# A three-stage kernel (attention, FFN, top-1 MoE): transposes moved to TensorE and to earlier places, row gathers issued a step ahead, another order of weight conversions and scatters

## The chip, the cores and the metric

The kernel runs on one core of a Trainium2 chip. The metric is the device time of one execution in microseconds (us). The figure for the kernel before is the median of three runs; the profile is of one execution, whose own time stands beside it below. Engines go by the profile's names: PE (TensorE), DVE (VectorE), ACT (ScalarE), POOL (GpSimd) and SP (SyncE, which only issues DMAs here).

## What is computed

```python
# 1. attention, 16 heads x 768 rows x 64; a row sees only keys of its own LSH bucket
scores = np.where(q_bucket[..., :, None] == k_bucket[..., None, :], q @ k.T / 8, -1e9)
x = softmax(scores) @ v                     # rearranged to 1536 tokens x 512

# 2. FFN, 512 -> 2048 -> 512, with a rational activation
h = x @ w_in
g = P3(h) / (1 + abs(b0) * abs(h) + abs(b1) * h * h + 1e-6)
x = g @ w_out

# 3. top-1 mixture of 8 experts, 512 -> 1024 -> 512
e_idx = np.argmax(x @ w_gate, axis=1)
gate_w = softmax(x @ w_gate)[rows, e_idx]
eom = sigmoid(x @ w_output_gate)
for e in range(8):
    mask = e_idx == e
    out[mask] = gate_w[mask, None] * eom[mask, e, None] * (np.maximum(x[mask] @ w1[e], 0) @ w2[e])
```

Which token goes to which expert is known only on the chip, after the last FFN tile.

## The kernel before

**Numbers.** Float32 matmuls are made of float16 parts: each operand is split into a high and a low half, and three products (high by high, high by low, low by high) are added up. Weights of the MoE arrive as float32 chunks of 128x1024 (512 KB) in eight buffers `st`. ACT converts a chunk into its high half `WH` (`conv_hi`, L1003), DVE then makes the low half `WL` (`conv_lo`, L1006). One expert has eight chunks, four for the up projection and four for the down projection.

**FFN.** Twelve tiles of 128 tokens go through `ffn_unit` and `ffn_end` (L663 to L679). `ffn_end` scales the result and splits it into halves (`X`, L667 on ACT, L668 on DVE), has it transposed by a DMA of SP (`x2T`), writes it to a scratch tensor `x2d`, and computes the gate logits on PE (L676, copied to `LG` by DVE, L679).

**Routing.** From the logits, `gating`, `early` and `final` give each token a slot. Slots are sorted by expert and lie in *pairs* of 2 x 128 rows (up to 12) and *rests* of 64 rows (up to 7). `inv(0)` on PE turns slots into row indices, DVE copies them as `idg` (for gathers, L936) and `idx` (for scatters). `SR` with numbers 1 and 2 (L940) and two more `inv` do the same for the scale of each row. Small one-row passes on DVE (L945 to L966) make registers and flags: which expert each pair and rest has, which pairs need new weights, how many pairs and rests there are. PE, SP, ACT, DVE and POOL load these flags. With this data there are 6 pairs (0 to 5) and 4 rests (0 to 3), and among the pairs after the first the expert changes once, at pair 4.

**Order.** All of the work up to pair 0 and the gather and transpose of pair 1 is a graph of operations; where each one stands is written down in the table `PLACES` (two characters for each operation), and the engines execute in that order. What follows, `tail`, is issued in the order in which its code is written. Each engine works strictly in its own order, so an instruction that waits holds up all that stand behind it on its engine.

**The tail.** Step `k` (1 to 5 here) works on pair `k` and rest `k-1`:

- POOL gathers rows of `x2d` into `XG` (L985): pair `k+1` and rest `k`. SP transposes `XG` to `XGT` (pairs) or `XRT` (rests) by DMA (L988).
- PE computes the hidden layer of the pair: `mm1` (L1020) for pairs 0 and 1, `up_pair` (L1078) for the others. ACT and DVE apply relu and split it into halves of `HT` (L1083, L1084). PE computes the output in `mm2s` (L1035). ACT scales it to `OS` (`scale_out`, L1039), POOL scatters it to the rows of `out` (`scatter`, L1043).
- SP loads the next weights (L792): the chunks of rest `k` by `load_rest`, and those of pair `k+1` by `load_pair` (its chunks are moved only if that pair's expert differs). ACT and DVE convert rest `k-1`'s chunks (`conv_rest`) between the pair's relus, and pair `k+1`'s in `renew`, under a flag.
- PE computes the rest in `rest(k-1)` (L1095 and L1108, relu `HTR` at L1098), and POOL scatters it (L1113).

In `step`, the gathers for the next step are issued at its start; in `whole(k)` the transposes stand between the two halves of `up_pair` (`turns(k)`), and the scatters of the pair stand at the end, after the next step's flag is known.

## Time and profile before

| | |
|---|---|
| median of 3 runs | 669.41 us (666.66, 669.41, 671.71) |
| profiled execution | 669.22 us, of which the span of the profile is 667.4 us |
| TensorE's granted clock, mean | 0.985 of full speed |
| busy: PE / DVE / ACT / POOL | 580.8 / 557.8 / 438.8 / 273.2 us |

The span runs from the first to the last instruction that the profiler recorded; 1.8 us of the execution lie outside. A clock of 1.00 is 2.4 GHz, one of 0.50 is 1.2 GHz. In a list of waits, the engine and line that waited stand first, and behind the arrow what ended the wait. In a timeline, brackets hold the idle time of the engine before an instruction.

### The profile page before, as it was taken

What the parts mean: (1) busy time and instruction counts of PE and PEld (TensorE: products, weight loads), DVE (VectorE), ACT (ScalarE), POOL (GpSimd) and SP (SyncE); (2) the same over time, 40 slices, a digit from 0 to 9 for tenths busy, and PEclk for the clock granted to TensorE, in tenths of its full rate; (3) what the DMA queues carried; (4) which work ended last, traced back from release to release, by engine and by line L of the source; (5) the groups of instructions that cost most, each with busy time, mean ns of one, the idle gap of its engine ahead of it and who ended that gap; (6) DMA issues with size and microseconds to landing.
All of it is one profiled execution on the core that took longest, in us unless ns stands there. A gap on an engine that the chain in (4) does not pass through costs nothing.

```text
span 667.4 us, 18493 instructions
## 1 busy us (share of the span) xinstructions
PE 580.8 (87%) x7243; PEld 419.3 (63%) x7243; DVE 557.8 (84%) x1183; ACT 438.8 (66%) x644; POOL 273.2 (41%) x219
## 2 busy tenths in 40 slices
PE   0129997999999999999899999999997969979993
PEld 0015786677777776777676777777575746737571
DVE  6999999999999999988999999999965357176652
ACT  4417769988887887888877877765811356176552
POOL 1000215676656736664656564631303103121431
PEclk9999999999999999999999999999999979979997
DMA  8877889998899999999879995744813886799535
GB/s 267 245 228 232 220 237 197 176 166 170 134 158 180 196 211 175 155 165 164 145 134 155 154 149 89 130 95 97 276 35 101 227 227 226 155 396 329 172 90 111
DMA packets 224147, 119.62 MB, mean 179 GB/s; under 512 B 201647, under 2 KB 206639, under 8 KB 224048
## 3 DMA queue, kind: packets, MB, share of 16 engines
q1 hardware_dynamic: 221296, 109.92, 75.4%
q0 software_dynamic: 2752, 8.39, 4.1%
q8 instruction: 60, 0.98, 0.6%
q14 instruction: 39, 0.32, 0.2%
HBM read 80.01 MB, written 6.82 MB: 130 GB/s over the span
## 4 chain that ended last, share of the span: by engine, by line
DVE 37%; DMA 20%; issue 16%; ACT 12%; PE 11%; POOL 3%; POOLq 0%; SPq 0%; DVEq 0%; ACTq 0%
DMA out<-OS,idx 10%; DVE sm L568 7%; DMA pT<-phl 5%; ACT p L576 3%; DVE tmp L648 3%; ACT phl L312 3%; DVE tmp L440 2%; PE bank L660 2%; DVE tmp L649 2%; DVE WL L443 2%; DVE tmp L441 2%; DVE tmp L650 2%; DVE tmp L653 2%; DVE tmp L655 2%; DVE bank L654 2%
## 5 line engine op out<-in xcount | busy, mean ns | idle before, releaser
L313 POOL TENSOR_TENSOR phl<-p,phl 128x768 f16<-128x768 f32 x80 | 135.9, 1706 | 87.0 <-ACT phl L312 42.4
L634 PE MATMUL bank<-XT,WH 128*128 128x128 f16 x1440 | 129.6, 219 | 2.1 <-DVE tmp L655 1.5
L634 PEld LDWEIGHTS <-WH 128*128 128x128 f16 x1536 | 119.9, 98 | 15.2 <-issue 2.7
L634 PE MATMUL bank<-XT,WL 128*128 128x128 f16 x720 | 124.9, 219 | 0.2 <-DVE sm L569 0.2
L576 ACT ACTIVATE p<-scb,sm 128x768 f32<-128x768 f32 x96 | 93.0, 986 | 21.3 <-DVE sm L570 13.6
L660 PE MATMUL bank<-WH,G 128*128 128x512 f16 x352 | 104.9, 379 | 0.0
L568 DVE TENSOR_REDUCE sm<-scb 128x1 f32<-128x768 f32 x96 | 90.3, 950 | 4.6 <-PE scb L562 3.1
L660 PEld LDWEIGHTS <-G 128*128 128x128 f16 x576 | 52.2, 97 | 51.1 <-POOL G L313 1.4
L1006 DVE SCALAR_TENSOR_TENSOR WL<-st,WH 128x1024 f16<-128x1024 f32 x56 | 66.8, 1233 | 20.3 <-ACT WH L1003 18.3
L634 PEld LDWEIGHTS <-WL 128*128 128x128 f16 x768 | 75.1, 98 | 0.3 <-DVE WL L443 0.3
L313 POOL TENSOR_TENSOR G<-tmp,G 128x512 f16<-128x512 f32 x39 | 46.9, 1205 | 60.4 <-ACT G L312 56.4
L1003 ACT ACTIVATE WH<-st 128x1024 f16<-128x1024 f32 x56 | 56.5, 1049 | 21.6 <-DMA st<-in_w 21.3
L660 PE MATMUL bank<-WL,G 128*128 128x512 f16 x176 | 66.7, 379 | 0.0
L1035 PE MATMUL bank<-WH,HT 128*128 128x512 f16 x192 | 59.8, 392 | 5.8 <-ACT HT L1083 3.8
L312 ACT ACTIVATE phl<-p 128x768 f16<-128x768 f32 x72 | 60.1, 839 | 6.9 <-DMA pT<-phl 6.0
L585 PE MATMUL bank<-VH,pT 128*128 128x65 f16 x528 | 55.2, 195 | 2.9 <-DMA pT<-phl 2.5
L586 PE MATMUL bank<-VL,pT 128*128 128x64 f16 x528 | 55.2, 192 | 0.0
L587 PE MATMUL bank<-VH,pT 128*128 128x65 f16 x528 | 55.1, 193 | 0.0
L585 PEld LDWEIGHTS <-pT 128*128 128x128 f16 x528 | 49.1, 97 | 8.7 <-DMA pT<-phl 4.8
L1035 PEld LDWEIGHTS <-HT 128*128 128x128 f16 x288 | 28.2, 100 | 40.6 <-issue 4.3
L562 PE MATMUL scb<-AK,AQ 128*128 128x384 f16 x192 | 46.8, 326 | 5.8 <-ACT p L576 5.2
L586 PEld LDWEIGHTS <-pT 128*128 128x128 f16 x528 | 48.9, 99 | 4.6 <-issue 0.7
(282 smaller groups left out, 1425.2 us busy)
## 6 DMA issues: line engine op xcount, KB each, us to landing
st<-in_w SPq DMA_DIRECT2D x92, 512.0 KB
tmp<-in_wio SPq DMA_DIRECT2D x32, 512.0 KB
qraw<-in_qt_ SPq DMA_DIRECT2D x12, 256.0 KB
x2d<-X SPq DMA_DIRECT2D x12, 256.0 KB
kraw<-in_kt_ SPq DMA_DIRECT2D x5, 384.0 KB
vr<-in_v SPq DMA_DIRECT2D x5, 384.0 KB
AQ<-BQ SPq DMA_DIRECT2D x24, 64.0 KB
pT<-phl SPq DMA_TRANSPOSE x88
```

The costliest lines, as they stand in the source:

```text
L312: g.op("ACT", c_act(n, 1), lambda: nc.scalar.activation(out=hi, in_=src, func=AF.Copy), r=rd, w=kh, prio=prio, tag=tags[0], alt=[("DVE", c ...
L313: f = lambda e: lambda: e.tensor_tensor(out=lo, in0=src, in1=hi, op=ALU.subtract)
L568: g.op("DVE", 0.865, lambda: nc.vector.tensor_reduce(out=s[:, 0:1], in_=sc, axis=AX.XY, op=ALU.max), r=kb, w=[("mx", ks)], prio=prio, tag= ...
L576: g.op("ACT", 0.975 if ac else 0.885, lambda: nc.scalar.activation(out=pf.rearrange("p (c n) -> p c n", c=2), in_=sc, func=AF.Exp, bias=s[ ...
L585: nc.tensor.matmul(o, lhsT=pt[:, k], rhs=VH[p][:, hh, k], start=(k == 0), stop=False)
L586: nc.tensor.matmul(o[:, 0:D], lhsT=pt[:, k], rhs=VL[p][:, hh, k], start=False, stop=False)
L587: nc.tensor.matmul(o, lhsT=pt[:, 6 + k], rhs=VH[p][:, hh, k], start=False, stop=(k == 5))
L634: nc.tensor.matmul(hp[:, j * 128:j * 128 + 128], lhsT=w_[:, f, d * 128:d * 128 + 128], rhs=xt[:, hl * 4 + d], start=(k == 0), stop=(k == 11))
L660: nc.tensor.matmul(bank_f32(abank), lhsT=G_[:, gl, c0:c0 + 128], rhs=w_[:, f, 512:1024], start=(f == 0 and k == 0), stop=(f == FT - 1 and ...
L1003: nc.scalar.activation(out=P["W"][p][0][c], in_=P["st"][c], func=AF.Copy, scale=512.0)
L1006: nc.vector.scalar_tensor_tensor(out=P["W"][p][1][c], in0=P["st"][c], scalar=512.0, in1=P["W"][p][0][c], op0=ALU.mult, op1=ALU.subtract)
L1035: nc.tensor.matmul(bank_f32(6 + sub), lhsT=P["HT"][sub][:, hl, f], rhs=w_[4 + f // 2][:, c0:c0 + 512], start=(f == 0 and n == 0), stop=(f ...
```

## The change

It has five parts.

1. In `ffn_end` the last tile's halves are transposed by eight matmuls against the identity matrix (four into bank 1, evicted by ACT, four into the accumulator's bank, evicted by DVE) instead of a DMA of SP.
2. `idg` becomes an input of the two products `SR` 1 and 2 and of the first of the small passes that make flags, so that the row indices come first on DVE; one relu of pair 0 is put behind `SR` 0.
3. Pair 1's gathered rows are transposed by TensorE (`turn_pe`, evicted by `turned`) instead of SP.
4. In the tail, gathers are issued one step further ahead (`fetch(k + 2, k + 1)` in `turns(k)`), the transposes of the next pair stand at the start of a step, and rest 0's loads stand ahead of its gather and transposes. Half 0's relus come before the first three conversions of a rest, half 1's after them; conversions 3 to 7 follow those. The scatters of a pair directly follow its scaling, ahead of the rest's scatter. From step 5 on each half is scaled and scattered when its `mm2s` are done. The branch that held only the last scatters is gone.
5. Four rows of `PLACES` are new, for the order of the graph part.

```diff
 PLACES = (
...
-    "z{z}!0!2!4!6!8wEw)wWxBv3v{wkvfwuw|uqwYx9vNwmxjwOxLx=v}w@x^u!w~xZvzxFxzxNxVxbxfxpx/xrxxx[x}y4yAy2yCyGyayoyyy:y~zFzTyKyMyOySygyuxlzBzRzXzd!Gzhzp!E!I!O!Q!S!U!a!ezn!W!K!i"
...
+    "z{z}!0!2!4!6!8!A!C!EwMxHwmx*v3v{w+vfw|xluqwox(vNw:yKwax^yqv}xbywu!xpyAvzx=yax{y6yCyGyQymySyYyuy$y<y@y:y]y|z9zHzNzRzXzdzhz1z3z5z7zDzLyMzbzfzjzl!Szpzv!Q!U!a!c!e!g!k!ozt!G!I!K!W"
...
-        g.op("SP", TR, lambda: nc.sync.dma_start_transpose(out=x2T[i], in_=x2.rearrange("p a b -> p (a b)")), r=[("X2h", i), ("X2l", i)], w=[("x2T", i)], dma=1.27, prio=pr, tag="xz")
+        kx2 = [("x2T", i)] if ti < TILES - 1 else [("x2T", i, hl) for hl in range(2)]
+        if ti < TILES - 1:
...
+        else:
+            for hl, b in ((0, 1), (1, abank)):
+                def tu(hl=hl, b=b):
+                    for d in range(4):
+                        nc.tensor.matmul(bank_f32(b)[:, d * 128:d * 128 + 128], lhsT=x2[:, hl, d * 128:d * 128 + 128], rhs=P["ident"], start=True, stop=True)
...
-        g.op("DVE", 0.42, lambda k=k: V.tensor_tensor(out=P["SR"][:, k], in0=P["SO"], in1=bc(VAL[:, :, k:k + 1], [128, TILES, NSLOT]), op=ALU.mult), r=["SO"] + [(kk, b_) for b_ in blks], w=[("SR", k)], prio=RT2)
+        g.op("DVE", 0.42, lambda k=k: V.tensor_tensor(out=P["SR"][:, k], in0=P["SO"], in1=bc(VAL[:, :, k:k + 1], [128, TILES, NSLOT]), op=ALU.mult), r=["SO", "idg"] + [(kk, b_) for b_ in blks], w=[("SR", k)], prio=RT2)
...
+    def turn_pe(sub):
+        for c in range(8):
+            nc.tensor.matmul(scb[c // 4][:, sub, 128 * (c % 4):128 * (c % 4) + 128], lhsT=P["XG"][2 + sub][:, c], rhs=P["ident"], start=True, stop=True)
+
+    def turned(sub, h):
+        o, b = P["XGT"][2 + sub][:, 4 * h:4 * h + 4].rearrange("p a b -> p (a b)"), scb[h][:, sub]
+        if h:
+            nc.vector.tensor_copy(o, b)
+        else:
+            nc.scalar.activation(out=o, in_=b, func=AF.Copy)
...
-        g.op("SP", TR, lambda sub=sub: turn(1, sub), r=[("XG", 2 + sub)], w=[("XGT", 2 + sub)], dma=1.27, prio=RT + 49)
+        if not sub:
+            g.op("PE", c_mm(128, 8), lambda: turn_pe(0), r=[("XG", 2), "ident"], w=[bkey(2), bkey(4)], prio=RT + 49)
...
+        def out_of(k, sub):
+            scale_out(k, sub), scatter(k, sub)
+
+        def first_pair():
+            for sub in range(2):
+                for half in range(2):
+                    mm1(1, sub, half)
+                    if not sub and not half:
+                        turn_pe(1), turned(1, 0), turned(1, 1)
+                        fetch(2, 1), turns(1)
+                    relu_hi(1, sub, half), relu_lo(1, sub, half)
+                conv_rest(0, 4 * sub, 4 * sub + 4)
+                load_pair(2, 4 * sub, 4 * sub + 4)
+
         def whole(k):
-            r = k - 1
-            if k > 1:
-                conv_rest(r, 0, 4)
-                load_pair(k + 1, 0, 4)
-                up_pair(k, 0)
-                turns(k)
-                up_pair(k, 1)
-            else:
...
-            conv_rest(r, 4, 8)
-            load_pair(k + 1, 4, 8)
-            for sub in range(2):
-                for half in range(2):
-                    mm2s(k, sub, half)
+            r, late = k - 1, k > 4
+            if k == 1:
+                first_pair()
+            else:
+                up_pair(k, 0)
+                conv_rest(r, 0, 3), load_pair(k + 1, 0, 3)
+                up_pair(k, 1)
+                conv_rest(r, 3, 4 if late else 8), load_pair(k + 1, 3, 4 if late else 8)
+            mm2s(k, 0, 0), mm2s(k, 0, 1)
+            if late:
+                out_of(k, 0)
+                conv_rest(r, 4, 8), load_pair(k + 1, 4, 8)
+            mm2s(k, 1, 0), mm2s(k, 1, 1)
+            if late:
+                out_of(k, 1)
+            else:
+                scale_out(k, 0)
...
+        def fetch(k, r):
+            if k < NB:
+                gather(k, 0), gather(k, 1)
+            if r < NR:
+                gather_rest(r)
+
         def turns(k):
             if k + 1 < NB:
                 turn(k + 1, 0), turn(k + 1, 1)
             if k < NR:
                 turn_rest(k)
+            fetch(k + 2, k + 1)
...
         def step(k):
             r = k - 1
-            if k + 1 < NB:
-                gather(k + 1, 0), gather(k + 1, 1)
             if k == 1:
-                gather_rest(0), turn_rest(0)
                 load_rest(0, 0, 8)
-            if k < NR:
-                gather_rest(k)
+                gather_rest(0)
+                turn_rest(0)
+            else:
+                turns(k)
...
             renew(k + 1, 0, 4)
             load_rest(k, 0, 4)
-            scale_out(k, 0), scale_out(k, 1)
+            if k < 5:
+                scale_out(k, 1)
+                scatter(k, 0), scatter(k, 1)
...
         def steps_from(k):
             step(k)
             if k + 1 == NB:
-                scatters(k)
-            elif k < 4:
-                load_rest(k, 4, 8), scatters(k), steps_from(k + 1)
-            else:
-                with tc.If(steps > k + 1) as more:
-                    load_rest(k, 4, 8), scatters(k), steps_from(k + 1)
-                with more.Else():
-                    scatters(k)
+                return
+            with tc.If(steps > k + 1) if k > 3 else ExitStack():
+                load_rest(k, 4, 8), steps_from(k + 1)
```

How this moves instructions, at three places. First SP, from its load of the flags (`fli`) to the first loads of rest 0 (`st` from `in_w1`, `regs` being the registers that name the expert). Before:

```order
L970 TENSOR_LOAD fli_7400
L970 ISA x8
L988 DMA_TRANSPOSE XGT1_7435<-XG2_7430 128x8x128
L988 DMA_TRANSPOSE XGT1_7435<-XG3_7431 128x8x128
L988 DMA_TRANSPOSE XRT0_7436<-XG4_7432 128x8x128
L978 TENSOR_LOAD regs_7397
L978 ISA x2
L978 TENSOR_LOAD regs_7397
L978 ISA x2
L792 ISA
L792 DMA st0_7420<-in_w1 128x1024
```

After:

```order
L983 TENSOR_LOAD fli_7400
L983 ISA x8
L991 TENSOR_LOAD regs_7397
L991 ISA x2
L991 TENSOR_LOAD regs_7397
L991 ISA x2
L805 ISA
L805 DMA st0_7420<-in_w1 128x1024
```

The two transposes of pair 1 (`XGT1`) are gone from SP, and that of rest 0 (`XRT0`) has moved from ahead of the eight loads to behind them.

Then POOL, from pair 0's second scatter on (`XG2` and `XG3` hold a pair's gathered rows, `XG4` and `XG5` a rest's; the L1043 and L1067 rows behind it are the scatters of pair 1). Before:

```order
L1043 DMA out_0<-OS1_7442,idx0_7383 1536x512
L985 DMA XG2_7430<-x2d_72,idg_7391 128x1024
L985 DMA XG3_7431<-x2d_72,idg_7391 128x1024
L985 DMA XG4_7432<-x2d_72,idg_7391 128x1024
L985 DMA XG5_7433<-x2d_72,idg_7391 128x1024
L1148 REGISTER_ALU
L1148 COMPARE_AND_BRANCH
L1148 UNCONDITIONAL_BRANCH x2
L1201 COMPARE_AND_BRANCH
L1113 DMA out_0<-OS2_7443,idx_7390 1536x512
```

After:

```order
L1067 DMA out_0<-OS1_7442,idx0_7383 1536x512
L998 DMA XG4_7432<-x2d_72,idg_7391 128x1024
L998 DMA XG2_7430<-x2d_72,idg_7391 128x1024
L998 DMA XG3_7431<-x2d_72,idg_7391 128x1024
L998 DMA XG5_7433<-x2d_72,idg_7391 128x1024
L998 DMA XG2_7430<-x2d_72,idg_7391 128x1024
L998 DMA XG3_7431<-x2d_72,idg_7391 128x1024
L998 DMA XG4_7432<-x2d_72,idg_7391 128x1024
L1169 REGISTER_ALU
L1169 COMPARE_AND_BRANCH
L1169 UNCONDITIONAL_BRANCH x2
L1067 DMA out_0<-OS0_7441,idx_7390 1536x512
```

Three more gathers (pair 3 and rest 2) now stand in step 1, and pair 1's scatters ahead of the rest's scatter.

Last ACT in step 2 (`WH` from `st` are conversions, `HT` from `scb0` and `scb1` the relus of `up_pair`'s halves 0 and 1). Before:

```order
L1003 ACTIVATE WH_148<-st0_7420 128x1024
L1003 ACTIVATE WH_148<-st1_7421 128x1024
L1003 ACTIVATE WH_148<-st2_7422 128x1024
L1003 ACTIVATE WH_148<-st3_7423 128x1024
L1083 ACTIVATE HT_7438<-scb0_70 128x512 x2
L1083 ACTIVATE HT_7438<-scb1_71 128x512 x2
L1003 ACTIVATE WH_148<-st4_7424 128x1024
L1003 ACTIVATE WH_148<-st5_7425 128x1024
L1003 ACTIVATE WH_148<-st6_7426 128x1024
L1003 ACTIVATE WH_148<-st7_7427 128x1024
```

After:

```order
L1110 ACTIVATE HT_7438<-scb0_70 128x512 x2
L1027 ACTIVATE WH_148<-st0_7420 128x1024
L1027 ACTIVATE WH_148<-st1_7421 128x1024
L1027 ACTIVATE WH_148<-st2_7422 128x1024
L1110 ACTIVATE HT_7438<-scb1_71 128x512 x2
L1027 ACTIVATE WH_148<-st3_7423 128x1024
L1027 ACTIVATE WH_148<-st4_7424 128x1024
L1027 ACTIVATE WH_148<-st5_7425 128x1024
L1027 ACTIVATE WH_148<-st6_7426 128x1024
L1027 ACTIVATE WH_148<-st7_7427 128x1024
L1063 ACTIVATE OS0_7441<-bank6_68,cs__7394 128x512
```

The relus of half 0 have moved ahead of all conversions, those of half 1 ahead of the fourth only.

## Rows read from the trace of the kernel before

**Rows 1.** The page, part 1: busy time, share of the span, instructions of each engine.

```profile
PE 580.8 (87%) x7243; PEld 419.3 (63%) x7243; DVE 557.8 (84%) x1183; ACT 438.8 (66%) x644; POOL 273.2 (41%) x219
```

**Rows 2.** Waits of PE, 440 to 668 us: total, times, longest, in us.

```profile
PE scb L1108 <- ACT HTR L1098: 5.0, 1, 5.0
PE bank L1035 <- ACT HT L1083: 3.8, 1, 3.8
PE scb L1020 <- DMA XGT<-XG: 2.3, 1, 2.3
```

**Rows 3.** Timeline of PE: start, us, instructions [idle before, releaser].

```profile
497.62 0.20 PE L676 MATMUL bank<-wgh,x2T 128*128 128x16 f16 x2
...
514.18 0.27 PE L1020 MATMUL scb<-XGT,WH 128*128 128x128 f16 x2 [2.27 <-DMA XGT<-XG]
...
535.25 0.22 PE L1095 MATMUL bank<-XRT,WH 128*128 128x64 f16 x2
...
548.24 0.39 PE L1078 MATMUL scb<-XGT,WH 128*128 128x256 f16 x2
...
574.69 0.39 PE L1078 MATMUL scb<-XGT,WH 128*128 128x256 f16 x2
...
608.73 0.39 PE L1078 MATMUL scb<-XGT,WH 128*128 128x256 f16 x2
...
636.24 0.39 PE L1078 MATMUL scb<-XGT,WH 128*128 128x256 f16 x2
...
656.23 0.38 PE L1035 MATMUL bank<-WL,HT 128*128 128x512 f16 x1
...
656.88 0.38 PE L1035 MATMUL bank<-WL,HT 128*128 128x512 f16 x1
```

**Rows 4.** Windows: length; busy PE, PEld, DVE, ACT, POOL; PEclk, DMA share, GB/s.

```profile
514.00:524.00 10.00, 9.82 (x176) 9.82 (x176) 2.08 (x3) 1.79 (x3) 4.03 (x4) 1.00 0.75 163
540.00:550.00 10.00, 6.77 (x41) 3.52 (x42) 2.73 (x4) 4.33 (x7) 0.00 (x0) 0.66 0.66 179
...
590.00:600.00 10.00, 9.63 (x33) 3.91 (x34) 8.42 (x10) 8.51 (x10) 1.67 (x2) 0.72 1.04 389
```

**Rows 5.** Timeline of ACT: a conversion in step 3, the last scaling.

```profile
600.24 1.06 ACT L1003 ACTIVATE WH<-st 128x1024 f16<-128x1024 f32 x1 [0.23 <-DMA st<-in_w]
...
657.34 0.69 ACT L1039 ACTIVATE OS<-bank,cs__7394 128x512 f32<-128x512 f32 x1 [3.74 <-PEq L1201]
```

**Rows 6.** Waits of SP's queue, 500 to 668 us: total, times, longest.

```profile
SPq L988 <- DMA XG<-x2d,idg: 46.2, 11, 10.5
```

**Rows 7.** Timeline of SP's queue: start, us, instructions.

```profile
510.87 2.67 SPq L988 DMA_TRANSPOSE XGT<-XG  x2
...
525.21 10.96 SPq L792 DMA_DIRECT2D st<-in_w  x12
...
574.74 15.33 SPq L792 DMA_DIRECT2D st<-in_w  x16
...
650.86 3.75 SPq L988 DMA_TRANSPOSE XGT<-XG  x2
```

**Rows 8.** Timeline of DVE: the last tile's low half, its logits, row indices, flags.

```profile
492.85 0.69 DVE L668 SCALAR_TENSOR_TENSOR X<-scb,X 128x512 f16<-128x512 f32 x1 [1.12 <-ACT X L667]
...
498.11 0.17 DVE L679 COPY LG<-bank 128x16 f32<-128x16 f32 x1 [3.14 <-PE bank L676]
...
506.53 0.19 DVE L936 TENSOR_SCALAR idg<-bank 128x31 int32<-128x31 f32 x1
...
508.20 0.28 DVE L966 CAST fli<-flc 1x4 int32<-1x4 f32 x1
```

**Rows 9.** Timeline of POOL: the last two scatters.

```profile
653.88 1.57 POOL L1043 DMA_INDIRECT out<-OS,idx  x1 [3.40 <-ACT OS L1039]
661.72 1.00 POOL L1043 DMA_INDIRECT out<-OS,idx  x1 [6.27 <-DMA out<-OS,idx]
```

**Rows 10.** Tile `OS`: time from issue to landing of its scatters.

```profile
DMA to landing us min/median/max: 2.0/3.3/7.1
```

More of the change, by code (lines that the diff above doesn't have):

```diff
@@ L677, in gm @@
                     k += 1
-        g.op("PE", c_mm(16, 12), gm, r=[("x2T", i), "wgh", "wgl"], w=[kPV], prio=pr)
+        g.op("PE", c_mm(16, 12), gm, r=kx2 + ["wgh", "wgl"], w=[kPV], prio=pr)
         g.op("DVE", 0.11, lambda: nc.vector.tensor_copy(LG[:, ti, :], GT), r=[kPV], w=[("LG", ti)], prio=pr)
@@ L1136, in conv_rest, with renew, whole, without @@
                 conv(1, c0, c1)
+        f_new, n_rest, n_pair, steps = flags
+        def renew(k, c0, c1):
+            if k < NB:
+                with tc.If((f_new & (1 << (k - 1))) > 0):
+                    conv(0, c0, c1)
+        def out_of(k, sub):
[10 more added lines that the diff above has]
+                load_pair(2, 4 * sub, 4 * sub + 4)
+        def whole(k):
+            r, late = k - 1, k > 4
[15 more added lines that the diff above has]
+                scale_out(k, 0)
+        def without(k):
+            conv_rest(k - 1, 0, 8)
+            load_pair(k + 1, 0, 8)
+        def fetch(k, r):
+            if k < NB:
+                gather(k, 0), gather(k, 1)
+            if r < NR:
+                gather_rest(r)
         def turns(k):
```

42 lines of the change are left out of this document (16 added, 26 removed).

## The prediction, made before the changed kernel was run

> **What bounds the kernel now.** I read the page first. TensorE is busy for 580.8 us of a span of 667.4 us [rows 1], so what matters is where it stands idle and where it runs slowly. The program is the same in both kernels up to the end of the last FFN tile, about 492 us into the span, so only the last 175 us can change. There I read the waits of TensorE [rows 2]: three waits stand out, 5.0 us on a relu of a rest (`HTR`), 3.8 us on a relu of a pair (`HT`) and 2.3 us on the transposed rows of pair 1 (`XGT`). Next the starts of the steps on TensorE's timeline [rows 3]. A step lasts from one pair's first matmul to the next one's: step 1 from 514.18 to 548.24 = 34.06 us, step 2 26.45, step 3 34.04, step 4 27.51, step 5 20.8 (to the last matmul at 656.88, and 0.2 more), then 10.3 us to the end of the span. Steps 1 to 4 hold the same matmuls, so step 2 shows what a step costs with nothing in the way, and steps 1 and 3 lose 7.6 us each. The windows [rows 4] say how: 5.0 us of step 1's excess is the wait, and most of the rest is the granted clock, 0.66 in 540 to 550 us and 0.72 in 590 to 600 us (a mixture of 1.2 and 2.4 GHz), so both idle times are followed by a stretch at half clock. After the wait of 2.27 us ahead of 514.18 the clock stayed at 1.00.
>
> Why TensorE waits is on ScalarE: the relus stand behind weight conversions, and these wait for `st`, that is for loads [rows 5]. The loads are issued by SP, in order, behind the transposes of gathered rows, and SP waited for gathers 46.2 us in 11 waits [rows 6]. Rest 0's first load is issued at 525.21, 11 us into its step; the loads for step 3 wait until 574.74, when step 3 has already begun [rows 7]. So the bound of this stretch is the start of the loads. The end of the span is bound by something else: the scatter issued at 653.88 has to land before the next can start, at 661.72, and that waits 6.27 us for it [rows 9].
>
> **The change, part by part.** All sums are made against the profiled run (span 667.4, run 669.22: 1.8 us lie outside the span). Its time is 0.2 us under the median of the three runs, 669.41.
>
> *Start: last tile, indices first, first pair by TensorE.* The last tile's transposition leaves SP: its low half is ready at 493.54 and its logits are copied at 498.11 [rows 8], 4.57 us. After: eight matmuls of 128 columns (176 such took 9.82 us [rows 4], so 0.45), two copies of 128x512 side by side (0.69 [rows 5]), three matmuls of mm2s that stand ahead of the gating on TensorE (656.23 to 656.88, so 0.65), the gating itself (from 497.62 to the copy, 0.5 [rows 3, 8]): 2.3 us, and I allow 0.8 for the handoffs between four engines, so 3.1: logits 1.5 us earlier. The row indices then follow at 505.65 instead of 506.53 [rows 8], less than 1.5 because the block `inv(0)` stands behind matmuls of pair 0. What is put behind them (the products SR1 and SR2 and the small passes that make the run flags) comes later by the length of what it moved past: I put the flags' cast, 508.20 in before [rows 8], at 510.0, and TensorE's load of them into registers at 511.0. The first pair's transposes on SP start at 510.87 and take 2.67 us [rows 7]; in their place stand 8 matmuls (0.45) and a copy (0.69), behind the flags on TensorE, so pair 1 begins at about 512.4 instead of 514.18 [rows 3]. Gain 1.8. Bounds: 0, if the gather of pair 1 or the flags come no earlier, and 3, if nothing but the matmuls lies between; I take the value near the middle, since both chains have a row.
>
> *Rest 0's loads first on SP.* They follow the flags instead of two transposes of pair 1 and one of rest 0, so they start at about 512.7 instead of 525.21, and at the pace of the loads of before (a conversion of 1.06 plus a wait of 0.23 us at 600.24, so 1.29 us each [rows 5]) the eighth lands near 524. The conversions end near 530. Rest 0 is reached at 535.25 in before [rows 3], at 533.5 after. The wait of 5.0 goes, and the half clock behind it. That leaves some 3 us before anything of rest 0 would be late again. Step 1 becomes 26.45 + 0.45 for the second sub-block's eight matmuls = 26.9 or 26.95: gain 7.1.
>
> *Gathers a step ahead, transposes at a step's start.* Transposes now find their rows landed (an indirect transfer lands in 7.1 us at most [rows 10], and a step has 26), so SP goes straight on to loads: those used in step 3 start near 560 instead of 574.74. The same transposes and gathers are issued, only earlier; each costs GpSimd 1.0 to 1.6 us [rows 9], at a place where it waits for nothing on this path. In step 3 the relu wait of 3.8 us and the slow stretch go. Left over is about 0.65 us, because `rest(2)` waits for a VectorE relu that stands behind the conversions of `renew(4)`. Step 3 becomes 27.1: gain 6.9. Step 4 comes to step 2's 26.45: gain 1.06. Step 2 had no loss: gain 0. The tightest point is pair 4: its new weights are done some 3 us ahead of their use.
>
> *Other order of relus and conversions.* Half 0's relus stand ahead of three conversions, half 1's behind them (before: four conversions ahead of all). With loads early this costs nothing, covered by the second half's matmuls; without that cover it is the slower rival below.
>
> *End.* The scatter issued at 653.88 was waited for until 661.72, with the transposes of the unused pair 6, issued from 650.86 on, beside it [rows 7, 9]; a landing took 2.0 us at least, 3.3 in the median, 7.1 at most [rows 10]. After, the transposes are done at the step's start and the scatter of the first half starts at about the same place, lands in 3.3 us (near 657.2 on the scale of before), and the second starts after its own scaling, 657.34 + 0.69 = 658.03 [rows 5], plus 0.1. So 661.72 - 658.12 = 3.6, of which I take 3.5. Bounds: 0, if the first still takes 7.1, and 3.6.
>
> Sum: 1.8 + 7.1 + 6.9 + 1.06 + 3.5 = 20.4. Span 667.4 - 20.4 = 647.0; with 1.8 outside 648.8, and 0.2 to the median: **649.0 us**.
>
> **A rule against it.** In before, the load pace was 1.29 us still at 600.24 [rows 5], in the 10 us in which DMA was busiest (share 1.04 [rows 4]), so the trace shows no slowing. The Trainium skill, "DMA: Bandwidth & Descriptors", section "Queues, rings and completion order", says that each DMA engine takes packets in turn from the queues that have work. By it three gathers of 256 KB each would push pair 4's loads back by up to their own bytes, an estimate of half a load each by the pace above, 1.9 us in all. That stays within the 3 us of margin, so by the rule the sum is the same but the second rival below is likelier than by the row.
>
> **Rivals.**
> 1. *Start and end give nothing* (chance 0.15). For it: the start hangs on two chains that are only 1 to 2 us apart, and a landing of 7.1 us was seen [rows 10]. Against it: the transposes beside the last scatter are gone. Time 649.0 + 1.8 + 3.5 = 654.3, about 654.
> 2. *Pair 4's weights come late* (0.15). Step 3 has both rest 2's loads and pair 4's, 16 loads of 1.29 = 20.6 us in a step of 26.5, and now gathers beside them, so up_pair(4) waits. If it waits as long as a relu does now, 3.8 us, and half clock costs as much again (7.6 - 3.8), step 3's gain is given back: 649.0 + 6.9 to 7.6, about 656.
> 3. *Slower: the relus of half 1 behind conversions that wait for loads* (0.04). On ScalarE these relus stand behind the first three conversions of a rest in every step 2 to 4. If loads are not earlier by the move (the three gathers are now ahead of the scatters on GpSimd, and the transposes on SP still wait for them), each of the four steps pays what step 3 pays now: 4 x 7.6 = 30.4 instead of 7.6 + 7.6 + 1.06 = 16.3, so +14.1, less 1.8 and 3.5 at the ends: about 678. It decides from the point at which the loads of a rest land over 3 us after up_pair's first half. Against it: by the order, nothing between the flags and rest 0's loads is left on SP, and gathers of a step have 26 us to land.
> 4. *The change does not do what it says* (0.06): loads start early, but conversions stay where they are because VectorE's half of them sets the pace, and only the end gains: 663 to 669, about 667.
>
> **How the numbers follow.** The forecast itself has 0.60; its own range is 645 to 652. Rivals 1 and 2 are faster too, and lie up to 656.6. Leaving out rivals 3 and 4 and the far edge of the others, the range is 644.5 to 659. A measurement of this kernel can tell about 1% from no change, 6.7 us, so faster means below 662.7: 0.60 + 0.15 + 0.15 and a part of rival 4, 0.91. Same is most of rival 4: 0.05. Slower is rival 3: 0.04.
>
> **What the changed profile would show.** Right: TensorE's waits from 440 us to the end lack the rows on `HTR` and `HT` of over 1 us; no window between 512 us and the end has a clock under 0.95; the first load of rest 0 is issued near 512.7, no transpose on SP waits long for a gather, steps 1 to 4 are 26.5 to 27.1 us each, and the last scatter waits for its own `OS` and not for another scatter. Wrong: a wait of TensorE on `WL` or `WH` at up_pair(4) (rival 2), a scatter waiting for `out` at the end (rival 1), a wait on `HT` in several steps (rival 3).

## The result, and the profile after

The changed kernel takes 664.74 us (median of 20 runs, 660.1 to 672.1) against 670.88 us before (median of 20 runs): a ratio of 0.9907, interval 0.9883 to 0.993. It is faster by 0.9%, not by the 3% of the forecast, and 664.74 lies outside the range of 644.5 to 659. The profiled execution took 666.15 us with a span of 664.3 us, 3.1 us less than before; a second profile of the same kernel, taken with the experiments, has a span of 663.2 us.

TensorE's waits from 440 us on (total, times, longest), to be held against [rows 2]:

```profile
PE scb L1135 <- ACT HTR L1125: 5.1, 1, 5.1
PE bank L1122 <- issue: 1.5, 3, 0.5
PE scb L1044 <- DVE XGT L1016: 0.8, 1, 0.8
```

The wait on the relu of a pair is gone, and one of 5.1 us on the relu of a rest (`HTR`) stands there as before. It is not the same wait. TensorE's timeline, as [rows 3]: the start of pair 1, the second sub-block's transposition (the first six of its eight matmuls) and the return to the pair, rest 0 and one of its gaps, pairs 2 and 3, the wait, pairs 4 and 5, the last matmul.

```profile
512.23 0.54 PE L1044 MATMUL scb<-XGT,WH 128*128 128x128 f16 x2 [0.46 <-ACT XGT L1018]
...
515.17 0.50 PE L1011 MATMUL scb<-ident,XG 128*128 128x128 f16 x6
...
517.00 0.27 PE L1044 MATMUL scb<-XGT,WH 128*128 128x128 f16 x2 [0.81 <-DVE XGT L1016]
...
535.40 0.22 PE L1122 MATMUL bank<-XRT,WH 128*128 128x64 f16 x2
...
537.50 0.19 PE L1122 MATMUL bank<-XRT,WL 128*128 128x64 f16 x1 [0.50 <-issue]
...
544.86 0.39 PE L1105 MATMUL scb<-XGT,WH 128*128 128x256 f16 x2
...
571.41 0.39 PE L1105 MATMUL scb<-XGT,WH 128*128 128x256 f16 x2
...
600.28 1.39 PE L1135 MATMUL scb<-WH,HTR 128*64 128x512 f16 x4 [5.06 <-ACT HTR L1125]
...
605.31 0.39 PE L1105 MATMUL scb<-XGT,WH 128*128 128x256 f16 x2
...
631.77 0.39 PE L1105 MATMUL scb<-XGT,WH 128*128 128x256 f16 x2
...
652.40 0.38 PE L1059 MATMUL bank<-WL,HT 128*128 128x512 f16 x1
```

The 5.06 us stand in step 3 now, where before the 5.0 us stood in step 1. Steps are counted as in the prediction, from one pair's first matmul to the next one's, and the last two columns are the second profile of the same kernel and the best kernel of the experiments:

| us | before | forecast | after | after, second profile | combined kernel |
|---|---|---|---|---|---|
| pair 1 begins | 514.18 | 512.4 | 512.23 | 512.75 | 512.64 |
| step 1 | 34.06 | 26.95 | 32.63 | 28.34 | 28.15 |
| step 2 | 26.45 | 26.45 | 26.55 | 26.45 | 26.46 |
| step 3 | 34.04 | 27.1 | 33.90 | 36.63 | 27.34 |
| step 4 | 27.51 | 26.45 | 26.46 | 26.53 | 26.46 |
| step 5, to the end of the last matmul | 21.0 | 21.0 | 21.0 | 21.0 | 21.0 |
| from there to the end of the span | 10.1 | 6.65 | 11.5 | 11.5 | 7.5 |
| span | 667.4 | 647.0 | 664.3 | 663.2 | 649.6 |

Pair 1's start is counted from the last tile's low half, whose row stands in [rows 8] for the kernel before. After:

```profile
493.20 0.69 DVE L668 SCALAR_TENSOR_TENSOR X<-scb,X 128x512 f16<-128x512 f32 x1 [1.12 <-ACT X L667]
```

The windows of the two slow places, with the columns of [rows 4]:

```profile
540.00:550.00 10.00, 10.00 (x95) 7.22 (x93) 1.30 (x3) 1.07 (x2) 1.31 (x2) 0.84 0.70 246
590.00:600.00 10.00, 5.22 (x108) 3.82 (x105) 5.50 (x6) 4.84 (x6) 2.00 (x1) 0.89 1.01 351
600.00:610.00 10.00, 9.61 (x67) 6.09 (x68) 4.91 (x7) 4.98 (x7) 2.32 (x2) 0.77 0.82 320
```

As before, a stretch at half clock follows idle time: the window has 0.84 after the gaps of rest 0, and 0.89 and 0.77 around the wait of 5.06 us (a mixture of the two levels).

Step 3 is read on SP and ACT. SP's queue:

```profile
512.75 4.91 SPq L805 DMA_DIRECT2D st<-in_w  x8
...
576.49 6.59 SPq L1001 DMA_TRANSPOSE XGT<-XG  x2
583.19 1.25 SPq L1001 DMA_TRANSPOSE XRT<-XG  x1
586.63 25.59 SPq L805 DMA_DIRECT2D st<-in_w  x16
```

ACT, the first four conversions of pair 4's new weights and, behind them, the relu of rest 2:

```profile
590.12 1.06 ACT L1027 ACTIVATE WH<-st 128x1024 f16<-128x1024 f32 x1 [0.24 <-DMA st<-in_w]
593.67 1.06 ACT L1027 ACTIVATE WH<-st 128x1024 f16<-128x1024 f32 x1 [2.49 <-DMA st<-in_w]
596.13 1.06 ACT L1027 ACTIVATE WH<-st 128x1024 f16<-128x1024 f32 x1 [1.40 <-DMA st<-in_w]
598.33 1.06 ACT L1027 ACTIVATE WH<-st 128x1024 f16<-128x1024 f32 x1 [1.14 <-DMA st<-in_w]
...
599.86 0.37 ACT L1125 ACTIVATE HTR<-bank 128x256 f16<-128x256 f32 x1
```

Rest 0's loads start at 512.75 as forecast. Pair 4's start only at 586.63, behind three transposes that end at 584.44, and their conversions start 2.2 to 3.6 us apart, where the kernel before had 1.29 [rows 5]. The relu stands behind them.

POOL at two places, the first gather of pair 3 and the last scatter:

```profile
533.22 1.00 POOL L998 DMA_INDIRECT XG<-x2d,idg  x1 [14.43 <-DMA XGT<-XG]
...
653.89 1.00 POOL L1067 DMA_INDIRECT out<-OS,idx  x1 [4.21 <-ACTq L1243]
```

The last scatter waits for its own data, as forecast (before, it waited for another scatter, [rows 9]). Yet the span goes on for 10.4 us. The view of the source lines shows what follows on POOL and SP: the last test of a flag (L1169; the last of the two times is the last start), on POOL the tests of semaphores that close the branch behind it (L1251), then the instructions that end the program (L1307; the one long drain is the first):

```profile
L1169 POOLq COMPARE_BRANCH  x12: 34/45/55, 535.1 to 655.2; - x12
L1169 SPq COMPARE_BRANCH  x12: 34/45/63, 540.0 to 658.3; - x12
L1251 POOLq EVENT_SEMAPHORE  x4: 17/43/43, 655.8 to 657.4; - x4
L1307 POOLq DRAIN  x3: 51/103/3247, 658.7 to 664.0; - x3
L1307 SPq EVENT_SEMAPHORE  x14: 17/28/28, 661.9 to 664.3; - x14
```

On both engines some 3.5 us lie between the last test and the first instruction that ends the program. I took them for a jump over the code that is not run; what fills them on POOL is read below, under the end.

### The profile page after: what moved, and what is told of

It is laid out like the page before. It is cut to its first block, busy times and chain, and to the rows that moved or that the text cites. A ratio compares the mean times of both kernels' runs of the same rounds, so it can differ in the third digit from the quotient of the medians.

```text
span 664.3 us, 18525 instructions
## 1 busy us (share of the span) xinstructions
PE 581.3 (88%) x7267; PEld 422.0 (64%) x7267; DVE 559.4 (84%) x1186; ACT 438.9 (66%) x647; POOL 278.8 (42%) x222
## 5 line engine op out<-in xcount | busy, mean ns | idle before, releaser
L1059 PE MATMUL bank<-WH,HT 128*128 128x512 f16 x192 | 57.1, 379 | 0.0
L998 POOL DMA_INDIRECT XG<-x2d,idg x23 | 30.4, 1321 | 53.6 <-DMA XGT<-XG 42.9
```

Of the source, the lines that this page charges most:

```text
L1059: nc.tensor.matmul(bank_f32(6 + sub), lhsT=P["HT"][sub][:, hl, f], rhs=w_[4 + f // 2][:, c0:c0 + 512], start=(f == 0 and n == 0), stop=(f ...
```

## The experiments

Edits are to the changed kernel unless it is said otherwise. "Step 3" and so on are read from TensorE's timeline as in the table above.

**1. Transposes behind loads.**

```diff
-                conv_rest(r, 3, 4 if late else 8), load_pair(k + 1, 3, 4 if late else 8)
+                conv_rest(r, 3, 4 if late else 8), load_pair(k + 1, 3, 4)
+                turns(k)
+                if not late:
+                    load_pair(k + 1, 4, 8)
...
-            else:
-                turns(k)
```

> The changed kernel, with the next pair's and rest's transposes on SP (and the gathers that follow them on POOL) put behind the first four loads of the next pair, in steps 2 to 5. Theory: step 3 of the changed kernel takes 33.9 us instead of 26.5 because pair 4's loads are issued only at 586.6, behind three transposes (576.5 to 584.4) and a load of registers, while their buffers are free from about 581; so the conversions of the renewal wait for loads (7.5 us in all), and the rest's relu behind them holds TensorE for 5.1 us, and half clock follows. Then pair 4's first load is issued before 583, the wait on HTR falls under 2 us, step 3 is 27 to 28.5 us, and the span about 6 us shorter than the changed kernel's 664.3. Rival: the loads are slow because gathers and a scatter are moved beside them (about 2.3 us for each chunk instead of 1.29); then an earlier issue gains 2 us at most, and step 3 stays over 31 us.

Measured: 679.11 us, ratio 1.0107 to before (1.004 to 1.0173): slower than both. The theory's own place came out as expected: step 3 is 27.34 us, and the wait on `HTR` is gone. But steps 1, 2 and 4 take 32.68, 33.10 and 33.61 us (step 1 is no longer than in the change), and the end takes 18.5 us instead of 11.5. TensorE's timeline, in rest 1:

```profile
564.90 0.22 PE L1122 MATMUL bank<-XRT,WH 128*128 128x64 f16 x2
...
571.25 0.21 PE L1122 MATMUL bank<-XRT,WL 128*128 128x64 f16 x1 [1.09 <-issue]
...
572.84 1.06 PE L1135 MATMUL scb<-WH,HTR 128*64 128x512 f16 x4
```

The up projection of a rest, 2.9 us elsewhere, takes 7.9. TensorE waits for no semaphore there ("issue"), which I read as a shortage of instructions. The gathers wait for the transposes, so they too had moved: POOL issued them at 565.43, 566.78 and 568.10, beside rest 1, and likewise beside rests 0 and 3; in the changed kernel rests 1 and 3 have no such gaps. At the end three gathers that nobody needs stood ahead of the scatters on POOL (657.74 to 662.85).

**2. The rest ahead of the renewal.**

```diff
-            renew(k + 1, 0, 4)
-            load_rest(k, 0, 4)
             if k < 5:
                 scale_out(k, 1)
...
                     rest(r)
+            renew(k + 1, 0, 4)
+            load_rest(k, 0, 4)
```

> The changed kernel, with the rest's work issued ahead of the first four conversions of the next pair's renewal, and the next rest's first loads behind that. Theory: the 5.1 us wait of step 3 comes from the relu of the rest standing behind conversions on ScalarE that wait for loads; without that order the wait on HTR goes. The loads are as late as before, so a wait on WH or WL at the next pair's first matmuls takes its place, 3 to 4.5 us, and step 3 and 4 together gain 1 to 3 us of the 7.4 lost. Rival: the wait on HTR has another cause (the transposed rows of the rest, or DVE); then it stays at about 5 us. A second rival: the conversions alone fit into the rest's time, no new wait appears, and 7 us are gained.

Measured: 668.96 us, ratio 0.9991 (0.9959 to 1.0023), no gain over before and slower than the change. The waits of TensorE:

```profile
PE scb L1105 <- ACTq L1169: 2.9, 3, 1.2
PE scb L1105 <- ACT WH L1027: 1.8, 1, 1.8
```

The wait on `HTR` went, so it does come from the order on ACT. As expected waits on `WH` and `WL` took its place (1.8 and 0.9 us). What I had not counted: ACT's test for the renewal (L1169), now behind the rest, ends waits of up_pair's first matmuls, 2.9 us in three steps. Steps 3 and 4 together take 61.6 us instead of 60.4, so in place of the expected gain of 1 to 3 us there was none.

**3. No loads for what does not exist.** Loads are left out for pairs from 6 and rests from 4, which this data does not have.

```diff
-            if k < NB:
+            if k < 6:
                 load(k, c0, c1)
...
-            if r < NR:
+            if r < 4:
                 load(NB + r, c0, c1)
```

> The changed kernel without the loads for pairs 6 to 11 and rests 4 to 6 (and the loads of their registers); with this data none of these exists, so no byte that is used is left out. Theory: the span ends 11.5 us behind the last matmul because SP still issues loads that move nothing until 658.04 and only then reaches the end; the last scatter is issued at 653.89 already. Then the last matmul is followed by the end of the span after 7.5 to 9 us, and the span is 2.5 to 4 us shorter. Rival: the end is set by the landing of the last scatter or by what follows it on POOL; then the distance stays at 11 to 11.5 us and the span is the same.

Measured: 663.75 us, ratio 0.9899 (0.9868 to 0.993). The distance from the last matmul to the end fell only from 11.5 to 10.4 us: SP was last by 1.1 us, and POOL is next. The same two lines of POOL in this kernel:

```profile
L1169 POOLq COMPARE_BRANCH  x12: 34/45/55, 535.7 to 653.8; - x12
L1307 POOLq DRAIN  x3: 45/103/3252, 657.2 to 661.0; - x3
```

From 653.8 to 657.2 POOL comes from the test to the end of the program, then it drains for 3.25 us. Taken for a jump, this gave the theory of experiment 5.

**4. Gathers of step 1 behind rest 0.**

```diff
         def turns(k):
...
-            fetch(k + 2, k + 1)
+            if k > 1:
+                fetch(k + 2, k + 1)
...
+            if k == 1:
+                fetch(3, 2)
             renew(k + 1, 4, 8)
```

> The changed kernel, with the gathers of pair 3 and rest 2 (three, which wait for SP's transposes until 533 and then run beside rest 0 on TensorE) put behind rest 0's scatter on POOL. Theory: rest 0's up projection takes 5.7 us instead of 2.9 because TensorE is short of instructions (four gaps of 0.7 us between 536.5 and 539) while these gathers and the pair's scatter land, and the half clock from 539.8 to 543 is the consequence; without the gathers there the gaps are gone, rest 0 takes 5.6 to 6 us in all instead of 9.5, and step 1 is about 29 us instead of 32.6. Rival: the gaps come from the jump over the flag ahead of rest 0 (code has to be brought in), whatever else is moved; then the gaps and the 9.5 us stay. In step 2 SP may wait 2 us for the gathers, which should cost nothing.

Measured: 665.46 us, ratio 0.9933 (0.9908 to 0.9958). Rest 0 on TensorE's timeline, and pair 2:

```profile
535.54 0.22 PE L1122 MATMUL bank<-XRT,WH 128*128 128x64 f16 x2
...
538.43 0.62 PE L1135 MATMUL scb<-WH,HTR 128*64 128x512 f16 x4
...
541.48 0.39 PE L1105 MATMUL scb<-XGT,WH 128*128 128x256 f16 x2
```

Rest 0 takes 2.89 us without a gap and 5.94 in all; step 1 is 29.16 us. But step 2 then took 29.05 (a wait of 1.27 us on `HT`, a gap of 0.48 in rest 1), so little was left of it in the sum: the expectation that the wait for the gathers in step 2 costs nothing was wrong. That rest 0 has no gap in one execution does not settle the theory, since three of eight executions with the gathers there have none either (experiment 11); that the gaps moved with the gathers in experiment 1 is the stronger sign.

**5. The last scatter in both branches** (on top of experiment 3).

```diff
-            if late:
-                out_of(k, 1)
-            else:
-                scale_out(k, 0)
+            scale_out(k, 1 if late else 0)
...
-            with tc.If(steps > k + 1) if k > 3 else ExitStack():
...
+                with tc.If(steps > k + 1) as more:
+                    load_rest(k, 4, 8), scatter(k, 1), steps_from(k + 1)
+                with more.Else():
+                    scatter(k, 1)
```

> The kernel without loads for absent pairs and rests, with the last scatter of a step from 5 on put back into both branches of the test for a further step, as the kernel before had it. Theory: behind the last scatter POOL now jumps over the code of the steps that are not run, 3.4 us from its branch (653.8) to its next instruction (657.2), then drains for 3.25 us; in the kernel before the jump lay ahead of the last scatters, under their waits. Then the distance from the last matmul to the end of the span falls from 10.4 us to about 7 and the span is about 3.4 us shorter than the 661.2 us without the branch. Rival: the landing of the scatter sets the end, and the jump is covered by it; then 10 us or more stay.

Measured: 660.61 us, ratio 0.9854 (0.9828 to 0.9879). The last matmul ends at 654.93, the span at 661.7: 6.8 us instead of 10.4. The span itself is no shorter than that of experiment 3, because pair 1 began 1.45 us later in this execution and rest 0 and step 3 lost more; the distance is what the edit touches. POOL's last scatter and drain:

```profile
655.98 1.03 POOL L1067 DMA_INDIRECT out<-OS,idx  x1 [4.15 <-ACTq L1240]
...
L1312 POOLq DRAIN  x3: 51/103/3735, 657.1 to 661.4; - x3
```

The drain begins 1.2 us behind the start of the scatter (657.14, 655.98), and not 4.7 us as in experiment 3 (657.17, 652.47). The time came out as expected, but it does not show the theory's jump: a wait for the landing of the scatter, which the edit moves under the drain, makes the same difference, and the landing times speak for it (see the end, below).

**6. Experiment 1 with the gathers at a step's end.** As 1, with `fetch(k + 2, k + 1)` taken out of `turns(k)` and put behind the rest at the end of `step(k)`.

> The changed kernel with the transposes behind the first four loads of the next pair (as in the first experiment, which was slower) and the three gathers of a step put to its end, behind the rest's scatter on POOL, instead of behind the transposes. Theory: the first experiment lost because its gathers ran beside rests 0, 1 and 3, where TensorE then was short of instructions (rest 1 took 12.3 us instead of 5.7) and fell to half clock; step 3 itself became 27.3 us as expected. With the gathers at the start of a step, beside the wide matmuls of up_pair, steps 1 to 4 take 29.2, 26.5 to 28, 27.3 and 26.5 to 28 us, and the span is 654 to 657 us. Rival: the gathers slow the loads of the next rest wherever they stand, the relus of half 1 wait behind conversions, and two or more steps stay over 30 us; then the span is 660 us or more.

Measured: 663.63 us, ratio 0.9909 (0.9883 to 0.9935). Steps 1 to 4 take 29.24, 27.95, 27.34 and 26.94 us, the theory's figures, and the last matmul ends at 645.27, 7.5 us earlier than in the changed kernel. The end then took 16.2 us: in the last step POOL still issues three gathers that nobody needs (649.07 to 652.7) and SP's loads run to 652.2; POOL closes the branch only when the last of these gathers has landed (656.23). The span of 661.5 lies in the range of the rival, but for another reason than the rival's; the steps fit the first theory.

**7. One part alone, on the kernel before:** rest 0's loads first.

```diff
+            if k == 1:
+                load_rest(0, 0, 8)
             if k + 1 < NB:
                 gather(k + 1, 0), gather(k + 1, 1)
             if k == 1:
                 gather_rest(0), turn_rest(0)
-                load_rest(0, 0, 8)
```

> The kernel before, with one part of the change alone: rest 0's eight loads stand ahead of its transpose on SP (and ahead of the gathers of step 1 in the code). Theory: the loss in step 1 of the kernel before is only the late start of these loads; the gathers stand where they were, at 515 to 520 us, long ahead of rest 0, so TensorE meets neither the wait of 5.0 us nor gaps, and step 1 falls from 34.06 to about 27 us, the span by about 7 us to 660.5. It gains more alone than the whole change. Rival: rest 0's transpose, now behind eight loads, comes late, or the first loads beside the gathers of pair 2 are slowed so that conversions are late all the same: then step 1 keeps 30 us or more.

Measured: 667.29 us, ratio 0.9958 (0.993 to 0.9986). The wait on `HTR` is gone and rest 0 has no gap. Yet step 1 is 30.27 us and not 27, half of the gain. TensorE's waits name the other half:

```profile
PE scb L1020 <- issue: 2.6, 6, 0.5
```

The loads and the gathers of pair 2 now run together, and the shortage of instructions came in pair 1's matmuls (519.5 to 523.1). In the kernel before the same gathers ran there without loads, and the matmuls had no gap.

**8. What the runs point to, combined.** Experiment 6; the last scatter in both branches; late loads and gathers inside the branch of the next step; and the second sub-block of pair 1 transposed through banks that `mm1` does not use:

```diff
+    def turn_bank(sub, h):
+        return bank_f32(7 if h else 1) if sub else scb[h][:, 0]
...
+                with tc.If(steps > k + 1) as more:
+                    load_pair(k + 1, 4, 8), load_rest(k, 0, 4)
+                    scatter(k, 1), fetch(k + 2, k + 1), renew(k + 1, 4, 8)
+                    load_rest(k, 4, 8), steps_from(k + 1)
+                with more.Else():
+                    scatter(k, 1)
```

> What the runs so far point to, in one kernel: transposes behind the first four loads of the next pair, gathers at a step's end behind the rest's scatter, the last scatter in both branches of the test for a further step, loads and gathers of a step that may not come inside that branch, and the second sub-block of pair 1 turned through banks 1 and 7, which mm1 does not use. Expected from the parts: from pair 1's first matmul (about 512) step 1 27.9 us (29.2 less the 1.3 us wait on the copies), step 2 28.0, step 3 27.3, step 4 26.9, step 5 22.7, end 6.8: a span near 652 us against 664.3 of the changed kernel and 667.4 of the kernel before, a median of 652 to 655 us. Rival: with the steps shorter the loads, at 8 chunks for each rest, are late again in step 3 or in the rests; then one of the steps stays over 31 us and the span at 656 us or more.

Measured: 650.93 us (649.08 to 653.95, 6 runs), ratio 0.9718 (0.9682 to 0.9754): 2.8% faster than before. TensorE's three longest waits from 505 us on:

```profile
PE scb L1138 <- DVE HTR L1129: 0.7, 1, 0.7
PE scb L1014 <- ACT OS L1066: 0.6, 1, 0.6
PE bank L1062 <- DVE HT L1055: 0.6, 1, 0.6
```

The steps are in the table above. The gain of 1.3 us on the copies came too: the second transposition and the return to `mm1` take 0.44 us (515.59 to 516.03) instead of 1.83.

**9 and 10. Step 3 without gathers, and without transposes.** Pair 5 and rest 4 (experiment 9), or pair 4 and rest 3 (experiment 10), are computed from older rows.

```diff
-            fetch(k + 2, k + 1)
+            if k != 3:
+                fetch(k + 2, k + 1)
```

for 9, and for 10:

```diff
-            if k + 1 < NB:
-                turn(k + 1, 0), turn(k + 1, 1)
-            if k < NR:
-                turn_rest(k)
+            if k != 3:
+                if k + 1 < NB:
+                    turn(k + 1, 0), turn(k + 1, 1)
+                if k < NR:
+                    turn_rest(k)
```

> The changed kernel without the three gathers of step 3; pair 5 and rest 4 are then computed from rows gathered earlier. It tells which of two makes pair 4's weights late in step 3. If it is the place of the transposes on SP, the first load still starts at 586.6 us and the wait on HTR stays over 3.5 us. If it is the traffic of the gathers beside the loads, chunks follow each other at 1.3 us instead of 2.3, the fourth conversion ends near 594.5 instead of 599.4, and the wait falls under 1.5 us.

> The changed kernel without the three transposes at the start of step 3 (pair 4 and rest 3 are computed from older rows; the gathers of the step then start at its beginning as well, since they wait for nothing). If the place of the transposes on SP makes pair 4's loads late, its first load starts before 583 us and the wait on HTR of 5.1 us is under 1.5 us. If the loads are late for lack of free buffers, they start at 586 us as before and the wait stays over 3 us.

Measured, one execution each: 9 took 657.79 us, 10 took 655.93. In 9 the loads start as late as before, 15.4 us into the step (583.35, step 3 from 567.97), the conversions follow each other at 1.4 to 1.7 us, and the wait is 1.8 us; step 3 is 28.88 us. So the order on SP alone does not make the wait: its threshold of 3.5 us was not met. ACT in 9, the second to fourth conversion:

```profile
588.59 1.06 ACT L1027 ACTIVATE WH<-st 128x1024 f16<-128x1024 f32 x1 [0.64 <-DMA st<-in_w]
590.25 1.06 ACT L1027 ACTIVATE WH<-st 128x1024 f16<-128x1024 f32 x1 [0.61 <-DMA st<-in_w]
591.65 1.06 ACT L1027 ACTIVATE WH<-st 128x1024 f16<-128x1024 f32 x1 [0.34 <-DMA st<-in_w]
```

In 10 SP goes straight on from the loads of the step before, and pair 4's first load is issued 9.7 us into the step (578.14, step 3 from 568.45) instead of 15.2, as soon as its buffer is free. The four conversions follow without a pause (586.86 to 590.83), TensorE's only wait there is 0.7 us on DVE, and step 3 is 27.39 us, though the gathers are issued as well (578 to 582.6):

```profile
578.14 21.20 SPq L805 DMA_DIRECT2D st<-in_w  x13
```

Both together make the loss: transposes ahead of the loads bring the start to where the gathers are, and the gathers then stretch them. Removing either leaves a wait of at most 1.8 us. Each is one execution, but in the five executions of kernels that have both in step 3 (the change twice, experiments 3 to 5) the step takes 32.4 to 36.6 us.

**11. The changed kernel again.**

> The changed kernel once more, unchanged, for a second profile. Theory: the losses of step 3 (wait on HTR of 4 to 5 us, step 33 to 34 us) and of the end (11 to 11.7 us behind the last matmul) are fixed by the order of the code and come again. The gaps of TensorE in rest 0 are a race: in the kernels run so far they came where the first gather of pair 3 was issued 2.0 us or more ahead of rest 0's first matmul (five kernels), and not where it was 1.8 us (two kernels); so they come again if that lead is 2.0 us or more, and step 1 is then 31.5 to 33 us, else 28.3. Rival: the gaps have nothing to do with that lead; then the two disagree.

Measured: 665.01 us. The wait on `HTR` is 7.2 us and step 3 36.63, somewhat beyond the range given; the end is 11.5 us. Rest 0 had no gap, and step 1 is 28.34 us:

```profile
534.03 1.07 POOL L998 DMA_INDIRECT XG<-x2d,idg  x1 [15.16 <-DMA XGT<-XG]
```

The lead of this gather over rest 0's first matmul (535.48) is 1.45 us. Over the eight executions with these gathers beside rest 0, gaps came at leads of 2.0 to 2.3 us (five) and none at 1.45, 1.8 and 1.8 us.

## Why the prediction was wrong, step by step

*Start: right.* Pair 1 began at 512.23 for 512.4. That it came so near holds some luck, since pair 1 begins anywhere from 511.1 to 514.4 in the eleven executions with the changed start; but that spread lies ahead of the last tile. From the start of the last tile's low half, pair 1 begins 21.3 us later in the kernel before (492.85, 514.18) and 19.0 in the changed one (493.20, 512.23), 19.0 to 19.1 in all eleven. The gain of this part is 2.3 us, for 1.8.

*Step 1: the mechanism was right, and two costs were missing.* The wait of 5.0 us went, as forecast: rest 0's conversions are done in time. "26.45 + 0.45 for the second sub-block's eight matmuls" was mis-sized: the eight matmuls, a gap between them and the wait on their copies take 1.83 us (515.17 to 517.00); experiment 8 shows 0.44 when they go through other banks. The second cost was not in the sum at all: TensorE had three gaps of 0.5 us in rest 0, with no semaphore to wait for, when the gathers of pair 3 ran beside it, and then half clock, some 4 us in all (32.63 against 28.34 us in the second profile). The sentence that failed is "each costs GpSimd 1.0 to 1.6 us [rows 9], at a place where it waits for nothing on this path": I counted the gathers' time on POOL and not whom they disturb. It came in five of the eight executions that have these gathers there.

*Step 3: the step that failed most.* "SP goes straight on to loads" holds for the rests' loads (560.59 for "near 560"). It fails for pair 4's: `turns(k)` at the start of a step puts three transposes and a register load, 10 us on SP, ahead of the loads that the step needs, where the kernel before had the first four loads ahead of them. The first load starts 5.5 us later by it (15.2 us into the step, 9.7 in experiment 10). The margin of 3 us was taken from loads that start as their buffers come free. Then the gathers, now beside these loads, stretched them: conversions start 2.7 us apart on average with them (590.12 to 598.33) and 1.6 without (experiment 9). Experiments 9 and 10 take the two apart. And "Left over is about 0.65 us" named the right place, the relu of rest 2 behind the conversions of `renew(4)`, and holds where the weights are there (0.7 us on VectorE in experiments 8 and 10); with late weights the wait is 5.1 us on ScalarE's relu (7.2 in the second profile), and it comes at rest 2 and not at up_pair(4), where rival 2 looked for it. Rival 2, given 0.15, had half of the cause, the gathers beside the loads, and not the transposes ahead of them; its price (step 3's gain given back) is what was measured.

The Trainium skill, "DMA: Bandwidth & Descriptors", section "Queues, rings and completion order", by which the gathers would hold the loads up, was the better guide here than the row of the kernel before: from the first to the end of the fourth conversion took 9.27 us with the gathers and 5.82 without (experiment 9), 3.45 us for the 1.9 estimated by it.

*Step 4 and step 5: right*, 1.05 for 1.06, and no change.

*End: the wait that was to go went, and two others took its place.* Forecast were 3.5 us of gain, with bounds of 0 and 3.6; measured was a loss of 1.4. The last scatter no longer waits for the one before it: it starts 1.1 us behind the end of the last matmul and not 4.5. What failed is the assumption that the 5.7 us behind the start of the last scatter stay as they are; they became 10.4. The branch that was removed stands among the edits and got no price. In the kernel before, the last scatter stood inside it (Else), and POOL closed the branch at 661.7 and began its drain at 662.8, while the scatter was landing:

```profile
L1212 POOLq EVENT_SEMAPHORE  x3: 17/43/43, 661.5 to 661.7; - x3
L1270 POOLq DRAIN  x3: 51/103/3490, 662.8 to 667.1; - x3
L1148 SPq COMPARE_BRANCH  x12: 34/45/63, 543.2 to 662.2; - x12
```

In the changed kernel it stands ahead of the last test, and POOL tests its semaphore when it closes the branch (L1251). The trace has the landing at 657.33, and the test that follows a pause of 1.4 us starts at 657.35; in experiment 3 these are 655.85 and 655.88, in experiment 6, where a gather is the last to land, 656.23 and 656.25. So POOL waits there for a landing, 3.4 us from the scatter's start, and then drains. It is not the jump that I took it for: from POOL's branch to its next instruction it is 0.4 us (655.39 to 655.83). Experiment 5 gives 3.6 us for the place of the scatter. The second wait is SP's. Its loads that move nothing bring it to its last test at 658.3, and experiment 3 gives 1.1 us for them. The last row above says more: in the kernel before SP came to that test only at 662.2, 5.2 us ahead of the end of the span, and in the changed kernel the end lies 6.0 us behind it. An earlier scatter alone would then have gained little; the sum priced the end by POOL alone.

Summed up from the profile: start 1.9 (2.3 less 0.35 by which the last tile came later in this execution), step 1 1.4, step 2 -0.1, step 3 0.1, step 4 1.1, end -1.4: 3.1 us. The chance that the time would change by less than 1%, 0.05, was far too low: it was tied to one rival, and the costs above came at four places, while each rival priced one or two of them alone. That gains of this size can be had is shown by experiment 8, whose 650.93 us are close to the 649.0 forecast; it is another kernel than the one forecast, with each of the four costs taken out by an edit of its own.

## What to carry to other kernels

When a transfer is moved earlier, write down what is moved past it on the same queue, and for each of those when its own consumer needs it: the transposes gained nothing by being early and made the loads behind them start 5.5 us later. Price moved gathers by whom they run beside, loads and dense streams of short matmuls above all, not by their time on POOL. And at the end of a kernel with branches, look at what an engine waits for when it closes the last one: here a scatter issued ahead of the branch had to land before POOL could go on, and one issued inside it did not. Before the end of a chain is priced, see which engine comes next behind it.

## What the runs showed of the hardware that I had not expected

TensorE can stand idle with no semaphore in the way: gaps of 0.5 us and more, mostly 0.72 to 0.77 us from one to the next, in stretches of short matmuls (64 or 128 columns) beside gathers issued by POOL. Loads alone did not do it: in the kernel before, rest 0 began at 535.25 beside loads and had no gap. Gathers without loads did it in rest 0 (64 columns): from 535.7 to 539.3 us, where the gaps of the changed kernel lie, all 216 packets in the trace are on the queue of POOL's transfers. They did not do it beside pair 1's matmuls of 128 columns in the kernel before (514.89 to 520.2, loads only from 525.21 on); experiment 7, with loads there as well, has six gaps, but pair 1 of the changed kernel, with both, has one of 0.25 us. Whether gaps come in rest 0 hung on a few tenths of a microsecond between gather and rest (experiment 11). The Trainium skill, "Runtime: NRT & Kernel Launch", section "Instruction fetch mechanics", says that an engine brings in its instructions through a DMA queue of its own, in blocks, and that this is mostly hidden; here it was not, if that is the cause. That the blocks wait behind the gathers is my guess, which no run here shows. That no transfer of instructions is among the 216 packets neither proves nor excludes it, and the cause of the gaps stays open.

Two transposes on SP's queue took 2.67 us where the queue was empty [rows 7] and 6.59 right behind loads.

When a branch is closed whose code is not run, POOL tests the semaphores of its transfers and waits for those that have not landed (3.4 us from the start of a scatter to its landing). On the other engines the last branch (L1251) of the changed kernel was followed by a pause of 2.5 us on SP, 3.0 on ScalarE and 3.5 on VectorE. The Trainium skill, "Runtime: NRT & Kernel Launch", section "Instruction fetch mechanics", says that a taken branch whose target has not been brought in has to wait for its code. These pauses would fit that and POOL's 0.4 us would not; no run here shows what fills them.
